# Planning four head-sum steps of block 1 later, one of them past the last LN2 apply of block 0

## The chip, the cores and the metric

The kernel runs on one core of one Trainium2 chip. The metric is device time in microseconds (us) of one execution. TensorE is the matrix engine (PE in the profile, its weight loads PEld), VectorE is DVE, ScalarE is ACT, GpSimd is POOL, and SyncE (SP) issues nearly all DMAs here (517 of 521 by the profile's list). PSUM is the memory that this kernel's matmuls write; the six buffers of its `acc` tiles are called banks here.

## The reference, cut to what matters

```python
x = A_x                                  # 2048 tokens x 1024, bfloat16
x = x + A_ref(layernorm(x), wqkv, wo)    # local dilated attention, 32 heads, 8 keys each
x = x + B_ref(layernorm(x), Wg, Wu, Wd)  # h = relu(gate) * up, 3584 wide, then down
x = x + A_ref(...)                       # both once more, same weights
x = x + B_ref(...)
```

The kernel works on blocks of 512 tokens. Four blocks for the first layer pair and four for the second make eight "blocks" n = 0 to 7. While TensorE runs the gate-up of block n, VectorE computes the attention of block n+1.

## The kernel before

Every piece of work is a closure with a planned time. They are emitted in the order of those times, and most of VectorE's work is chained in that order (`dv` issues each after the last). The planned time is thus only an order: nothing waits for a clock.

The attention scores of one block are a "head sum": products q*k over eight channel groups c, added up, in two halves h. A step is one product and one addition:

```python
def mult(h, c):                # one head-sum step; t has 2 buffers, ac has 1
    def f():
        ...
        dv(nc.vector.tensor_tensor, t[:], i0, i1, op=ALU.mult)   # product
        if c > 1:
            add(h, c - 1)                                        # sum of the step before
        if c == KC - 1:
            add(h, c)
    return f
# steps: [mult(h, c) for h in range(2) for c in range(8)]; so step 6 is h=0, c=6
```

LN2 of block 0 normalizes four tiles; the gate-up of block 0 needs all four, transposed by DMA. Tiles 1 to 3 are done on VectorE: statistics, then `rstd` on GpSimd (a pow), then the apply.

```python
nc.gpsimd.tensor_tensor(rstd[:], vpe[:], neg_half[:, 0:1], op=ALU.pow)   # in the statistics
...
dv(nc.vector.tensor_scalar, xn[:, t, :], x_tile, mv[:, 0:1], rstd[:],    # the apply
   op0=ALU.subtract, op1=ALU.mult)
```

The gate-up allocates its PSUM tiles from six banks; `relu(gate)` has three buffers `r`, and VectorE's multiply `hT` frees both the up bank and an `r`:

```python
for nm in ("g", "u"):
    acc = psum.tile([P, BLK], F32, tag="acc", name=f"acc_{nm}")      # 6 banks
    ... 8 matmuls of 128x128 by 128x512 ...
    if nm == "g":
        rs[j] = pool["hid"].tile([P, BLK], BF16, tag="r", name="r", bufs=3)
        nc.scalar.activation(rs[j][:], acc[:], ACT.Relu)
def gate(j):
    dv(nc.vector.tensor_tensor, hold["hT"][:, j, :], ups.pop(j)[:], rs.pop(j)[:], op=ALU.mult)
```

Weights come in 1 MB slabs through five buffers. The kernel chains what SyncE issues in the order of the plan (`sp_dma`), their loads with nearly all other transfers: `store_s` and `load_s`, which take the head sums through DRAM, stand in this queue too.

Of the kernel before, what the change touches and what calls it, by code (L numbers as in the profile page):

```python
# [36 lines left out]
def kernel(  # L37
# [553 lines left out]
    def prod_sum_steps(n):  # L591
        st = att[n]

        def mult(h, c):
            def f():
                if h == 0 and c == 0:
                    st["s"] = big_tile([P, TPB, W, P], f"s_{n}")
                i0, i1 = qk_bcast(n, c, WH * h, WH)
                if c == 0:
                    t = work.tile([P, WH, BLK], F32, tag="ac", name=f"ac_{n}_{h}", bufs=1)  # L600
                    st["ac"] = t
                else:
                    t = work.tile([P, WH, BLK], F32, tag="t", name=f"t_{n}_{h}_{c}")
                    st[("t", c)] = t
                if n < NB:
                    dv(nc.vector.tensor_tensor, t[:], i0, i1, op=ALU.mult)
                else:
                    nc.vector.tensor_tensor(t[:], i0, i1, op=ALU.mult)  # L608
                if c > 1:
                    add(h, c - 1)  # L610
# [4 lines that stand above are left out]
        def add(h, c):  # L615
            ac, t = st["ac"], st.pop(("t", c))
            o, i0, i1 = ac[:], ac[:], t[:]
            if c == KC - 1:
                o = _ap(st["s"], WH * h * P, [[P, WH], [W * P, TPB], [1, P]])
                i0, i1 = (i[:].rearrange("p w (q t) -> p w q t", t=P) for i in (ac, t))  # L620
            if n < NB:
                dv(nc.vector.tensor_tensor, o, i0, i1, op=ALU.add)
            else:
                nc.vector.tensor_tensor(o, i0, i1, op=ALU.add)  # L624

        return [mult(h, c) for h in range(2) for c in range(KC)]
# [258 lines left out]
    def spread(steps, at, gap):  # L885
        for i, f in enumerate(steps):
            ev.append((at + gap * i, f))
# [37 lines left out]
    t_fill = t_wo0 + GRP * KC  # L925
# [54 lines left out]
    sums1 = prod_sum_steps(1)  # L980
    spread(sums1[:4], t_pv0 + 34.5, 4.5)
    spread(sums1[4:6], t_wo0 + 0.5, 2.5)
    spread(sums1[6:10], t_fill + 1.4, 4.6)
    spread(sums1[10:], t_gu0 + 2.6, 5.4)
    spread(load_v_steps(1), t_wo0 + 4.0, 7.0)
    ev.append((t_gu0 - 0.01, start_hidden))
# [107 lines left out]
```

## Time and profile before

| | before |
|---|---|
| median of three executions | 1617.8 us |
| the profiled execution, a further one, as timed | 1618.55 us |
| its span in the profile | 1616.8 us |
| PE busy | 1610.6 us |
| granted clock | 1.00 |

The profile page of the kernel before, its busy times (engine, us, share of the span, instructions) and the chain of work that ended last:

```profile
PE 1610.6 (100%) x7689; PEld 789.5 (49%) x7689; DVE 1138.9 (70%) x964; ACT 473.4 (29%) x964; POOL 180.5 (11%) x168
...
PE 99%; DMA 1%; DVE 0%; ACT 0%; issue 0%; POOL 0%; DVEq 0%; SPq 0%; ACTq 0%
```

The waits of PE in the kernel before (who waited for whom: total us, times, longest). This is the whole list:

```profile
PE scratch L132 <- DVE ones L309: 1.5, 1, 1.5
PE tp L386 <- DVE xn_first L106: 0.6, 1, 0.6
PE acc_wo L132 <- DMA w_o<-in_A_wo_dram: 0.6, 1, 0.6
```

PE lacked work for 2.7 us, all before 162 us, and the change acts at 180 us. While it works, its groups of eight matmuls start every 1.7263 us, 215.8 ns for each matmul, and of the gate and up groups that the timeline of this trace lists whole, none starts sooner than 1.72 us after the one before it. With no wait left where the change acts, the question is whether it makes a new one; it cannot remove one.

The timeline of VectorE in the kernel before, at the change (start, duration, operation):

```profile
180.24 0.15 DVE L106 TENSOR_SCALAR vpe<-mv 128x1 f32<-128x1 f32 x1
180.32 2.29 DVE L106 TENSOR_TENSOR t<-q,k 128x2048 f32<-128x2048 bf16 x1
182.53 2.28 DVE L106 TENSOR_TENSOR ac<-ac,t 128x2048 f32<-128x2048 f32 x1
184.73 0.54 DVE L106 TENSOR_SCALAR xn_b<-x,mv,rstd 128x1024 bf16<-128x1024 bf16 x1
...
200.85 1.28 DVE L106 TENSOR_TENSOR hT<-acc_u,r 128x512 bf16<-128x512 f32 x2
```

`vpe` is the variance of tile 3, `t` and `ac` the product and sum of step 6, `xn_b` the apply, and the first two `hT` come at 200.85. GpSimd's pow for tile 3, in its timeline:

```profile
180.48 2.54 POOL L300 TENSOR_TENSOR rstd<-vpe,neg_half 128x1 f32<-128x1 f32 x1 [3.49 <-DVE vpe L106]
```

It takes 2.54 us beside the product, against 0.55 us for each of tiles 1 and 2. The timeline of PE, with the first gate and up groups (no idle bracket: no wait):

```profile
190.45 1.89 PE L132 MATMUL acc_g<-xnT_b,w_g 128*128 128x512 bf16 x8
192.17 1.89 PE L132 MATMUL acc_u<-xnT_b,w_u 128*128 128x512 bf16 x8
```

The fifth gate group (starting at 204.26) takes the PSUM bank that the first `hT` frees. And the fifth up slab is issued, and first used, here (SyncE's timeline, then PE's):

```profile
236.78 0.39 SPq L121 DMA_DIRECT2D w_u<-in_B_W_up_dram  x1
...
247.43 1.89 PE L132 MATMUL acc_u<-xnT_b,w_u 128*128 128x512 bf16 x8
```

This load landed 9.2 us after issue by the trace, at 246.0: 1.4 us before its first use.

### The profile page before, as it was taken

To read this page: it belongs to the slowest core of one execution; us is meant where nothing else is said; L and a number is where in the kernel's file an instruction comes from. 1 tells how busy PE (TensorE), PEld (TensorE's weight loads), DVE (VectorE), ACT (ScalarE), POOL (GpSimd) and SP (SyncE) were. 2 spreads that over 40 slices of the span, in tenths; PEclk is the share of its full clock that TensorE was granted. 3 is DMA by queue.
4 is the path that set the end of the run, shared out by engine and by line. 5 is a ranking of instruction groups with operands and counts; after the bars stand their busy time and mean duration, and the time that the engine had idled before them with its cause. 6 is when DMAs were issued, how large, how long until landed. Compare 5 with 4: busy or idle time off the path is not lost.

```text
span 1616.8 us, 19042 instructions
## 1 busy us (share of the span) xinstructions
PE 1610.6 (100%) x7689; PEld 789.5 (49%) x7689; DVE 1138.9 (70%) x964; ACT 473.4 (29%) x964; POOL 180.5 (11%) x168
## 2 busy tenths in 40 slices
PE   9999999999999999999999999999999999999999
PEld 6646544444444445444454444544445444444445
DVE  6999979996989698929389293893939939311211
ACT  4753312132116313603136031361313311131110
POOL 3400100010003002300053000530005100000000
DMA  9767857596659666784747847489574874655452
GB/s 308 180 189 249 213 165 254 183 216 204 208 192 226 192 184 211 192 246 147 227 158 201 241 153 229 154 202 255 161 229 156 206 240 156 210 162 175 156 169 66
DMA packets 359065, 317.94 MB, mean 197 GB/s; under 512 B 105024, under 2 KB 332736, under 8 KB 358464
## 3 DMA queue, kind: packets, MB, share of 16 engines
q1 hardware_dynamic: 358272, 315.87, 67.2%
q8 instruction: 60, 0.98, 0.3%
q10 hardware_dynamic: 704, 0.85, 0.2%
q14 instruction: 29, 0.24, 0.1%
HBM read 266.29 MB, written 34.66 MB: 186 GB/s over the span
## 4 chain that ended last, share of the span: by engine, by line
PE 99%; DMA 1%; DVE 0%; ACT 0%; issue 0%; POOL 0%; DVEq 0%; SPq 0%; ACTq 0%
PE acc_u L132 24%; PE acc_g L132 24%; PE dacc L132 18%; PE acc_v L132 7%; PE acc_q L132 7%; PE acc_wo L132 7%; PE acc_k L132 6%; PE dacc_pair L132 6%; DMA w_o<-in_A_wo_dram 1%; DMA x<-in_A_x_dram 0%; PE tp_pair L386 0%; DVE x L848 0%; DVE bst L103 0%; DVE bst L106 0%; ACT kst L540 0%
## 5 line engine op out<-in xcount | busy, mean ns | idle before, releaser
L132 PE MATMUL acc_u<-xnT_b,w_u 128*128 128x512 bf16 x1792 | 423.3, 379 | 0.0
L132 PE MATMUL acc_g<-xnT_b,w_g 128*128 128x512 bf16 x1792 | 423.3, 379 | 0.0
L793 ACT ACTIVATE r<-acc_g 128x512 bf16<-128x512 f32 x224 | 133.6, 596 | 728.7 <-PE acc_g L132 699.4
L106 DVE TENSOR_TENSOR hT<-acc_u,r 128x512 bf16<-128x512 f32 x224 | 150.9, 686 | 241.7 <-PE acc_u L132 239.1
L132 PE MATMUL dacc<-w_d,hT 128*128 128x512 bf16 (+2 forms) x1428 | 302.0, 371 | 0.0
L132 PEld LDWEIGHTS <-hT 128*128 128x128 bf16 x1876 | 181.3, 98 | 206.0
L132 PEld LDWEIGHTS <-w_u 128*128 128x128 bf16 x1792 | 175.3, 98 | 211.4
L132 PEld LDWEIGHTS <-w_g 128*128 128x128 bf16 x1792 | 175.3, 98 | 211.4
L106 DVE TENSOR_TENSOR pv<-a,vhm 128x4096 bf16<-128x4096 bf16 x64 | 143.5, 2284 | 0.0
L848 DVE TENSOR_TENSOR x<-dacc,x 128x512 bf16<-128x512 f32 (+2 forms) x39 | 24.5, 659 | 154.3 <-PE dacc L132 154.3
L608 DVE TENSOR_TENSOR t<-q,k 128x2048 f32<-128x2048 bf16 x56 | 128.0, 2292 | 6.7 <-ACT k L543 4.6
L106 DVE TENSOR_TENSOR t<-q,k 128x2048 f32<-128x2048 bf16 x56 | 127.5, 2286 | 3.7 <-ACT k L543 2.6
L106 DVE TENSOR_TENSOR pv<-pv 128x1024 bf16<-128x1024 bf16 (+1 forms) x128 | 113.7, 950 | 0.0
L132 PE MATMUL acc_wo<-w_o,oT 128*128 128x512 bf16 x512 | 112.0, 379 | 0.6 <-DMA w_o<-in_A_wo_dram 0.6
L549 POOL COPY kh<-k 128x14 bf16<-128x14 bf16 x40 | 56.0, 1405 | 504.1 <-ACT k L543 504.1
L624 DVE TENSOR_TENSOR ac<-ac,t 128x2048 f32<-128x2048 f32 x48 | 109.7, 2284 | 0.3
L106 DVE TENSOR_TENSOR ac<-ac,t 128x2048 f32<-128x2048 f32 x48 | 109.7, 2284 | 0.0
L263 POOL TENSOR_TENSOR st_b<-st_b,neg_half 128x1 f32<-128x1 f32 x29 | 43.9, 1521 | 526.6 <-ACT st_b L262 526.6
L132 PE MATMUL dacc_pair<-w_d,hT 128*128 128x512 bf16 (+1 forms) x448 | 95.9, 366 | 0.0
L132 PEld LDWEIGHTS <-oT 128*128 128x128 bf16 x512 | 50.0, 98 | 61.2 <-DMA w_o<-in_A_wo_dram 1.1
L258 ACT ACTIVATE xn_b<-x 128x1024 bf16<-128x1024 bf16 x29 | 30.3, 1045 | 127.8 <-DVE x L106 65.7
L446 ACT CAST vT<-acc_v 128x512 bf16<-128x512 f32 x56 | 32.7, 586 | 57.3 <-PE acc_v L132 56.3
(136 smaller groups left out, 1228.0 us busy)
## 6 DMA issues: line engine op xcount, KB each, us to landing
w_g<-in_B_W_gate_dram SPq DMA_DIRECT2D x56, 1024.0 KB, 7.4
w_u<-in_B_W_up_dram SPq DMA_DIRECT2D x56, 1024.0 KB, 5.5
w_d<-in_B_W_down_dram SPq DMA_DIRECT2D x48, 1024.0 KB, 6.2
w_o<-in_A_wo_dram SPq DMA_DIRECT2D x16, 1024.0 KB, 8.1
vhm<-v_d SPq DMA_DIRECT2D x32, 284.0 KB, 6.7
v_d<-vT SPq DMA_DIRECT2D x8, 1024.0 KB, 10.0
oT<-o_d SPq DMA_DIRECT2D x32, 256.0 KB, 3.7
w_d<-in_B_W_down_dram SPq DMA_DIRECT2D x16, 512.0 KB, 3.9
```

What stands on the lines that cost most here:

```text
L106: tail_dve[0] = f(*args, **kwargs).ins
L132: tail_pe[0] = nc.tensor.matmul(*args, **kwargs).ins
L258: nc.scalar.activation(xn, xt[:], ACT.Square, accum_out=sq)
L263: nc.gpsimd.tensor_tensor(rstd, vpe, neg_half[:, 0:1], op=ALU.pow)
L446: tail_act[0] = nc.scalar.copy(st["vT"][:, c, :], acc[:]).ins
L549: nc.gpsimd.tensor_copy(khalo[n][:, c, :], k[:, BLK:BLK + HALO])
L608: nc.vector.tensor_tensor(t[:], i0, i1, op=ALU.mult)
L624: nc.vector.tensor_tensor(o, i0, i1, op=ALU.add)
L793: tail_act[0] = nc.scalar.activation(rs[j][:], acc[:], ACT.Relu).ins
L848: run = dv if n < NB - 2 else (lambda f, *args, **kwargs: f(*args, **kwargs))
```

## The change

The intent: let the last LN2 apply, which gate-up waits for, go ahead of head-sum work that nobody needs soon. The whole diff:

```diff
-    spread(sums1[6:10], t_fill + 1.4, 4.6)
+    spread(sums1[6:10], t_fill + 3.3, 4.0)
```

Tile 3's statistics are planned at `t_fill + 0.1` and its apply at `t_fill + 3.1`. Of the four shifted steps only step 6 crosses another event. Compared in the built programs, PE's order, waits and PSUM banks do not change; on VectorE one apply moves ahead of one product and one sum.

## The prediction

> What bounds the kernel. TensorE is the whole span. The page shows PE busy 1610.6 of 1616.8 us (100%), the chain of waits is 99% PE, and the granted clock is 1.00. Groups of eight 128x512 matmuls start every 1.7263 us in the timeline (215.8 ns each)[...]. The waits of PE list 2.7 us in all: 1.5 (first ones), 0.6 (first transpose), 0.6 (a wo slab, at 161 us). From 165 us to the end the list of PE's waits is empty. Nothing after that point is left for a schedule to win.
>
> What the change does. Compared instruction by instruction, the programs have the same instructions, PSUM banks, TensorE order and TensorE waits. Only one thing moves: on VectorE the LN2 apply of tile 3 (0.54 us) now comes before the product (2.29 us) and sum (2.28 us) of head-sum step 6, instead of after. The other shifted steps keep their places.
>
> Costs, from the timeline at 180 us. Before, the apply's rstd (a POOL pow) is waited for under those two operations: variance at 180.24, product 180.32, sum 182.53, apply 184.73 to 185.27, transpose issued 185.30 and landed 3.2 us later at 188.5. The first gate-up matmul starts at 190.45 without waiting, so the old order had about 1.9 us of slack. After, the apply waits for the pow as tiles 1 and 2 do (0.73 and 0.66 us idle), runs at about 181.1 and ends at about 181.7. Its transpose goes out when the queue gets to it, an estimate of 184 to 185, no later than before: 0.5 to 1.5 us more slack where there was enough. The pow itself, 2.54 us beside the product in the old order and 0.55 us for tiles 1 and 2, should be about 0.55 us again[...].
>
> The price: those 0.7 to 0.8 us of VectorE idle push all later VectorE work back (step 7 from 185.19 to about 186.0, the first gate multiply hT from 200.85 to about 201.6), until VectorE's idle time at 232 to 243 us (2.8 us before each hT) absorbs it. Does PE feel it? By the programs' PSUM banks, the matmul group that starts at 204.26 needs the first hT, which ended at 201.53: 2.7 us of slack, the smallest of this stretch; the others have 2.9 to 6.6 us. The relu that takes the first r buffer again, at 202.73, has 1.2 us. All exceed 0.8. The head-sum halves reach DRAM about 0.8 us later, and the head sum starts at 243.12 behind an hT, with attention's output not needed before 311 us. So on the critical path: 0.0 us.
>
> Prediction: 1617.8 us, unchanged; range 1617.2 to 1618.6 (8 in 10), which is run-to-run scatter (before: 1617.72 to 1617.87) and a small stall unseen. Chances: faster by over 2% 0.00, within 2% 0.99, slower by over 2% 0.01.
>
> What would show it right: PE waits the same 2.7 us, none after 165 us; the gate-up's first matmul still at 190.45; apply 3 at about 181.1 with 0.7 us idle on POOL rstd; that pow near 0.55 us; first hT 0.7 to 0.8 us later; hT back on its old times by 235 us.
>
> What would make it wrong: an earlier transpose that collides with other DMA and lands after 190.4; a slack in PSUM or the r buffers smaller than read; a VectorE delay that lasts past 232 us and reaches block 1's output projection at 311 us; or a chip with another scatter.

The forecast's sum, 0.0 us on the critical path, keeps all its terms: PE's empty list of waits, the 0.7 to 0.8 us of idle, and the slacks of 1.9, 2.7 and 1.2 us. That the pow would take 0.55 us rests on tiles 1 and 2 alone.

## The result, and the profile after

| | before | after |
|---|---|---|
| median (6 executions each) | 1618.03 us | 1618.16 us |
| lowest to highest | 1617.72 to 1618.36 | 1617.87 to 1618.61 |

The ratio is 1.0001 (95% interval 0.9988 to 1.0014): the same. Ratios here are the mean time of one kernel's fast runs over that of the other's in the same rounds, so not quite the ratio of the medians quoted.

All of PE's waits after the change:

```profile
PE scratch L132 <- DVE ones L309: 1.5, 1, 1.5
PE tp L386 <- DVE xn_first L106: 0.2, 1, 0.2
```

Nothing waits after 165 us, as before. The wait of 0.6 us for a `w_o` slab is gone from this trace, but that is not the change's doing: the programs are identical up to there. It makes PE 0.68 us earlier at 190 us than in the trace of the kernel before, and the times of the two profiled executions (1617.87 against 1618.55) differ by just that. The trace of the kernel before is thus of a rather late execution. Compare times of the two traces with that in mind.

VectorE at the change:

```profile
180.35 0.15 DVE L106 TENSOR_SCALAR vpe<-mv 128x1 f32<-128x1 f32 x1
181.16 0.55 DVE L106 TENSOR_SCALAR xn_b<-x,mv,rstd 128x1024 bf16<-128x1024 bf16 x1 [0.66 <-POOL rstd L300]
181.62 2.28 DVE L106 TENSOR_TENSOR t<-q,k 128x2048 f32<-128x2048 bf16 x1
183.83 2.29 DVE L106 TENSOR_TENSOR ac<-ac,t 128x2048 f32<-128x2048 f32 x1
...
201.81 1.28 DVE L106 TENSOR_TENSOR hT<-acc_u,r 128x512 bf16<-128x512 f32 x2
```

The apply runs 3.6 us earlier, and VectorE pays 0.66 us of idle for it, since the pow is no longer hidden. GpSimd's pow and the first gate group on PE:

```profile
180.58 0.55 POOL L300 TENSOR_TENSOR rstd<-vpe,neg_half 128x1 f32<-128x1 f32 x1 [3.49 <-DVE vpe L106]
...
189.77 1.89 PE L132 MATMUL acc_g<-xnT_b,w_g 128*128 128x512 bf16 x8
```

The transpose of tile 3 went out at 183.66 instead of 185.30 us and landed by 187.5 instead of 188.5, in front of a matmul that did not wait in either trace. The first `hT` is 0.96 us later. Two things got closer to a wait. ScalarE's relu waits for an `r` buffer, from the list of all waits of each kernel, before:

```profile
ACT r L793 <- DVE hT L106: 3.3, 1, 3.3
```

and after:

```profile
ACT r L793 <- DVE hT L106: 23.3, 7, 4.9
```

And the fifth up slab after the change, on SyncE and on PE:

```profile
238.45 0.39 SPq L121 DMA_DIRECT2D w_u<-in_B_W_up_dram  x1
...
246.75 1.89 PE L132 MATMUL acc_u<-xnT_b,w_u 128*128 128x512 bf16 x8
```

It landed 7.9 us after issue, at 246.35: 0.4 us of slack where there had been 1.4. Not all of this is the change's: the slab was issued 1.67 us later, PE is 0.68 us earlier in this trace, and a transfer that was 1.3 us faster gave most of it back. With the 9.2 us of the trace before it would have landed 0.9 us after its first use (an estimate from these figures).

One measure leaves out all that differs ahead of the change: the time from PE's first gate-up group to its last group of all. Its last group starts here, before and after:

```profile
1612.54 1.05 PE L132 MATMUL dacc<-w_d,hT 128*128 128x256 bf16 x12
```

```profile
1611.87 1.05 PE L132 MATMUL dacc<-w_d,hT 128*128 128x256 bf16 x12
```

That makes 1422.09 us before (from 190.45) and 1422.10 us after (from 189.77). This measure is called the stretch below. An earlier transpose could win only ahead of it, and there is nothing: from the start of the k groups ahead of the gate-up, at 173.18 and 172.51, to its first group are 17.27 and 17.26 us, ten groups at PE's spacing. It shows in one trace what the scatter of the times hides.

### The profile page after: what moved, and what is told of

It reads as the page before. It is cut to its first block, busy times and chain, and to the rows that moved or that the text cites. A ratio compares the mean times of both kernels' runs of the same rounds, so it can differ in the third digit from the quotient of the medians.

```text
span 1616.2 us, 19042 instructions
## 1 busy us (share of the span) xinstructions
PE 1611.0 (100%) x7689; PEld 789.7 (49%) x7689; DVE 1139.0 (70%) x964; ACT 473.4 (29%) x964; POOL 178.5 (11%) x168
## 4 chain that ended last, share of the span: by engine, by line
PE 99%; DMA 0%; DVE 0%; issue 0%; SPq 0%; ACT 0%; DVEq 0%
PE acc_u L132 24%; PE acc_g L132 24%; PE dacc L132 18%; PE acc_v L132 7%; PE acc_k L132 7%; PE acc_q L132 7%; PE acc_wo L132 7%; PE dacc_pair L132 6%; DMA x<-in_A_x_dram 0%; PE tp_pair L386 0%; DVE x L848 0%; PE L L132 0%; DVE xnT_first L106 0%; PE tp L386 0%; DVE xn_first L106 0%
```

## The experiments

Three theories were put up before the runs. S (slack): the earlier transpose and the later VectorE each stay inside a slack of PE, so neither shows. C (cancel): both show, and they cancel. I (indifferent): VectorE's order never matters here. A fourth, D, came out of the first runs. The four groups of runs (the first four, the next three, the next four, the last) were on different chips, each with its own runs of the kernel before. No kernel here computes anything wrong: the useless VectorE work writes a scratch tile.

### The changed kernel again

No edit.

> The changed kernel once more, with more rounds. Theory S (slack: nothing the change moves is on TensorE's path): ratio to before 1.000, within 0.0003; TensorE's waits empty after 165 us. Theory C (cancel: an earlier transpose wins about 0.8 us and the later VectorE loses about 0.8 us) also says 1.000. Theory I (indifferent: the order on VectorE never matters here) says the same; the next runs tell them apart.

Measured: 1618.77 us median (5 runs, 1617.68 to 1618.99) against 1618.03 for before (9 runs, 1617.62 to 1618.86), ratio 1.0003 (0.999 to 1.0015). PE's waits were again 1.5 and 0.2 us, both early. The means differ by 0.5 us (1618.53 to 1618.07), too little for the interval; a third set is below. The stretch is 1422.09 us (189.57 to 1611.66), as in the kernel before. But the slab was at the edge in this trace: issued at 238.45, it landed at 246.35, 0.2 us before its first matmul at 246.55, and the weight load ahead of that matmul did wait for it, as the timeline of the weight loads (PEld) shows:

```profile
246.38 1.56 PEld L132 LDWEIGHTS <-w_u 128*128 128x128 bf16 x8 [0.17 <-DMA w_u<-in_B_W_up_dram]
```

The matmul itself was not late.

### The delay without the earlier apply

To the kernel before, right after tile 3's apply:

```diff
+    def spend():
+        xt = x_tiles[3]
+        for w in (512, 128):
+            junk = stat_pool.tile([P, 6], F32, tag="junk", name="junk")
+            dv(nc.vector.bn_stats, junk[:], xt[:, 0:w])
+    ev.append((t_fill + 3.2, spend))
```

> The kernel before, with the apply of tile 3 in its old place and about 0.8 us of useless VectorE work (two bn_stats, 512 and 128 wide) right after it: the loss of the change without its earlier transpose. S: 0.0 us (within 0.3), first hT near 201.6 us as in the changed kernel, no TensorE wait after 165 us, more relu waits for hT as in the changed kernel. C: 0.8 us slower than before. I: 0.0.

Measured: 1618.12 us median, ratio 1.0000 (0.9987 to 1.0012). The added work took 0.88 us, and the relu waits for `hT` rose to 17.4 us in 5 waits. The interval alone, about 2 us either way, could not exclude C's 0.8 us. The trace does: PE's list has no wait after the start, and the stretch is 1422.25 us, 0.16 us more than before. One detail pointed ahead: the fifth up slab was issued at 238.4 and landed after 8.8 us, at 247.2, and its first group started at 247.26, 0.14 us later than PE's spacing of 1.73 us would have it. PE's list of waits did not show it; in the list of all waits the weight load waits 0.5 us for the slab.

### The apply between product and sum

```diff
                 dv(nc.vector.tensor_tensor, t[:], i0, i1, op=ALU.mult)
+                if (n, h, c) == (1, 0, 6):
+                    ev3[0]()            # the apply of tile 3, not issued at t_fill + 3.1 any more
                 if c > 1:
                     add(h, c - 1)
```

(The diff is cut to its core and shown at the call.)

> The apply stands between the product and the sum of step 6: earlier than before by one sum, with most of the wait for the pow hidden under the product. The pow should take about 2.5 us again beside the product (as in the kernel before), so the apply waits about 0.3 to 0.5 us and starts near 183.0 us. S: 0.0 us (within 0.3). C: faster than before by 0.3 to 0.8 us. I: 0.0.

Measured: 1617.80 us median, ratio 0.9999 (0.9986 to 1.0012). The timelines of VectorE and GpSimd in this run:

```profile
182.99 0.55 DVE L106 TENSOR_SCALAR xn_b<-x,mv,rstd 128x1024 bf16<-128x1024 bf16 x1 [0.44 <-POOL rstd L300]
...
180.41 2.54 POOL L300 TENSOR_TENSOR rstd<-vpe,neg_half 128x1 f32<-128x1 f32 x1 [3.48 <-DVE vpe L106]
```

The pow took 2.54 us again as soon as a product ran beside it, and the apply waited 0.44 us for it, where it had waited 0.66: the bubble is partly hidden. The times (means 0.16 us below the kernel before, standard error 0.17) can't exclude C's 0.3 us, but the trace does: the k groups ahead of the gate-up take 17.26 us here too, and the stretch is 1422.10 us. Nothing was won, and nothing could be, as PE's first gate-up group did not wait in the kernel before. So C has lost both its halves.

### A fourth relu buffer

```diff
-rs[j] = pool["hid"].tile([P, BLK], BF16, tag="r", name="r", bufs=3)
+rs[j] = pool["hid"].tile([P, BLK], BF16, tag="r", name="r", bufs=4)
```

> The changed kernel with 4 buffers for the relu output r instead of 3. The new waits of ScalarE for hT (23.3 us in 7 waits after the change, 3.3 us in 1 before) should fall to 5 us or less. S: the time stays as it is (within 0.3 us), since PSUM banks hide the late relus. If these waits cost anything, this run is faster than the changed kernel by it. The pool hands out PSUM banks a little differently in this build.

Measured: 1618.16 us median, ratio 1.0000 (0.9986 to 1.0014). The relu waits for `hT` fell from 23.3 us in 7 waits to 2.9 us in 1. Against the changed kernel in the same rounds (1618.77, means 0.45 us apart with a standard error of 0.28) the times leave open whether a few tenths were won; the stretches don't, 1422.10 us here and 1422.09 there. The most visible new wait of the changed kernel cost nothing in these traces.

### Two steps ahead of the apply

To the kernel before:

```diff
-    spread(sums1[6:10], t_fill + 1.4, 4.6)
+    spread(sums1[6:8], t_fill + 1.4, 0.8)
+    spread(sums1[8:10], t_fill + 10.6, 4.6)
```

> The kernel before with steps 6 and 7 of the head sum both ahead of the apply of tile 3: 6.9 us more VectorE work before it, so the apply starts near 191.6 us and its transpose lands near 195. S: TensorE stands at the first gate-up matmul (190.45 us before) for 4.5 to 5.2 us, and the time rises by about that, to 1622.3 to 1623.5 us; the transfers of k queued behind the transpose may add up to 2 us. C: the rise equals the whole delay of the transpose, about 6.9 us. I: no rise.

Measured: 1625.91 us median against 1617.89, ratio 1.0050. I falls: the place of the apply matters as soon as the transpose is late enough. PE's timeline in this run:

```profile
195.43 3.57 PE L132 MATMUL acc_g<-xnT_b,w_g 128*128 128x512 bf16 x8 [5.50 <-issue]
198.79 2.29 PE L132 MATMUL acc_u<-xnT_b,w_u 128*128 128x512 bf16 x8
200.93 1.89 PE L132 MATMUL acc_g<-xnT_b,w_g 128*128 128x512 bf16 x8
```

The transpose was issued at 192.25 and landed 3.1 us later, at 195.35; the profile names no releaser for the wait, but the start follows it by 0.1 us. The rise is 8.0 us, more than S said. Against an unstalled start at 189.77 the first group is 5.7 us late, and then two groups run slow: 3.36 and 2.14 us from start to start instead of 1.73, 2.0 us more. Together that is 7.7 us. The time alone would speak for C, whose 6.9 us is nearer than S's range; but the trace has one stop, of S's kind, and then slow matmuls (631 ns where they take 379), while the granted clock averaged 0.77 from 188 to 203 us, and 1.00 from 203 to 213 us. S had the place right and left the slow matmuls out.

### 3.0 and 6.0 us of useless VectorE work

To the changed kernel, the same `spend` with `(512,) * 5` and `(512,) * 10`. The early apply stays where it is.

> The changed kernel with 3.0 us of useless VectorE work (five bn_stats) after the early apply: VectorE is 3.8 to 4.0 us later than in the kernel before, the transpose is not. S: the slack of 2.7 us (the first hT ends 201.5, the fifth gate group starts 204.3 in its PSUM bank) is passed by 1.1 to 1.9 us; TensorE waits that long once, for hT, at that group, and nowhere else; the time rises by 1.0 to 1.9 us. C: the rise is 3.0 to 3.9 us. I: no rise.

> As the last, with 6.0 us (ten bn_stats), VectorE 6.8 to 7.0 us later than in the kernel before. S: one TensorE wait of 4.1 to 5.0 us at the fifth gate group, time up by about that, 3.0 us more than with 3.0 us of work: past the slack each us of VectorE costs one of the kernel. C: rise of 6 to 7 us. I: no rise.

Measured: 1620.61 us and 1624.55 us against 1617.89: 2.7 and 6.7 us more. PE's waits after the start, with 3.0 us of work:

```profile
PE acc_g L132 <- DVE hT L106: 1.8, 1, 1.8
```

and PE's timeline with 6.0 us:

```profile
208.55 3.19 PE L132 MATMUL acc_g<-xnT_b,w_g 128*128 128x512 bf16 x8 [4.74 <-DVE hT L106]
211.57 1.89 PE L132 MATMUL acc_u<-xnT_b,w_u 128*128 128x512 bf16 x8
```

The wait is the one foretold, for `hT`, at the fifth gate group and of the foretold size. The times are above S's range. With 6.0 us the remainder is the slow group (3.02 us to the next, 1.3 us too long; the granted clock averaged 0.83 from 203 to 213 us). With 3.0 us no group is slow. The trace has a second small loss: the up group expected at 248.87 us started at 249.09, when the fifth up slab landed (issued 241.14, 7.9 us). The two make 2.2 us (1.9 from start to start, and 0.2) in an execution of 1620.24 us, the fastest of the four, 2.35 above the median of before; the stretch grew by 2.17 us, so nothing else was lost. With 6.0 us it grew by 6.21 us, which the wait (4.9 us from start to start) and the slow group make up. This gave theory D: the late head-sum half holds SyncE's queue, and with it the slab behind it. (SyncE waited 13.5 us for `s` in this trace with 3.0 us of work, against 10.8 us in the kernel before, and issued the store at 234.21 instead of 230.09 us.) The rise of 6.7 us also lies in C's range; there the trace decides, not the time.

### Weight slabs ahead of the head-sum loads

To the kernel with 3.0 us of work, and to the changed kernel:

```diff
-            ev.append((at + 40.5, load_s(1)))
+            ev.append((at + 42.0, load_s(1)))
```

> 3.0 us of useless VectorE work as before, which raised the time by 2.6 to 2.7 us where one PSUM wait explains 1.9, with the four loads of the head sum's halves moved in the DMA queue behind the two weight slabs that stood after them. Theory D (a second path: the late head-sum half holds the in-order DMA queue, and the fifth up slab behind it lands too late): rise falls to 1.8 to 2.2 us, TensorE waits once, 1.8 us at the fifth gate group, and the up group at 249 us no longer starts late (0.2 us in the trace before). Theory S alone (PSUM is the only slack): nothing changes, 2.6 us.

> The changed kernel with the same reordering of the DMA queue. D: the fifth up slab, issued at 238.4 us in the changed kernel and landed 0.2 to 0.4 us before its first use, is issued near 231 us and lands over 4 us before it; the time is the same as the kernel before or lower by up to 0.3 us (1617.7 to 1618.0), as the changed kernel may lose 0.1 to 0.4 us in some runs there. S: same time as the changed kernel.

Measured: 1624.22 and 1621.23 us against 1618.26, so 6.0 and 3.0 us slower, not faster. This expectation failed in the time. In the changed kernel with slabs first, the slab did come early (issued 233.30, landed 6.3 us later, against 246.7 needed), but the head-sum loads behind two 1 MB slabs landed late (the median landing of the transfers that write or read the head sum there went from 5.2 to 11.9 us). VectorE's timeline there:

```profile
250.56 2.29 DVE L106 TENSOR_TENSOR u<-s 128x2048 f32<-128x2048 bf16 x1 [8.09 <-DMA s<-s_d]
```

In the changed kernel that sum starts at 243.36. The kernel chains VectorE's work in order, so the `hT` behind it are late too (the next at 254.03 us; in the changed kernel at 246.83), and PE's waits become:

```profile
PE acc_u L132 <- DVE hT L106: 2.3, 2, 1.2
...
PE acc_wo L132 <- DVE x L106: 1.0, 1, 1.0
```

These waits are the loss: listed they are 3.3 us, and the stretch grew by 3.8. The two transfers pull against each other, and the order of the kernel before is the better one. Because the edit opened this other wait, the times of these two runs do not test how much of the 2.7 us was the slab. The trace of the first does, which D had asked for: with 3.0 us of work and the slab early (issued 236.44, landed 6.6 us later), the up group came on PE's spacing, at 248.79 after 247.06, while the wait at the fifth gate group stayed (1.8 us). So the 0.2 us there had been the slab.

### 1.2 and 4.2 us of useless VectorE work

`spend` with `(512,) * 2` and `(512,) * 7`, in the changed kernel.

> The changed kernel with 1.2 us of useless VectorE work (two bn_stats). PSUM alone (S): the first hT comes at most 0.2 us too late for the fifth gate group, rise 0.0 to 0.2 us. D: the fifth up slab lands about 1.2 us later than in the changed kernel, where 0.4 us was left; TensorE waits 0.5 to 0.9 us there; rise 0.5 to 1.2 us. C (no slack): rise 1.2 to 2.1 us.

> The changed kernel with 4.2 us of useless VectorE work (seven bn_stats). With 6.0 us the fifth gate group waited 4.7 us and then ran slow (3.0 us to the next group instead of 1.7)[...]. Here the wait should be 2.9 to 3.1 us: S and D: no slow group, next group 1.73 us later, rise 3.1 (S) or 3.2 to 4.0 us (D, with a late slab); if it runs slow, the slow groups come with any wait of 3 us. C: rise 4.2 to 5.1 us.

Measured with 1.2 us: 1619.70 us median against 1618.26, ratio 1.0007 (0.9995 to 1.002). The five runs fall in two groups, 1618.49 and 1618.60, and 1619.70 to 1619.85. The profile fell in the slower group, and PE's list of waits has the line that D asked for:

```profile
PE acc_u L132 <- DMA w_u<-in_B_W_up_dram: 1.1, 1, 1.1
```

The slab was issued at 239.43 and took 9.1 us. At the fifth gate group PE lost 0.15 us only. The rise, 1.4 us by the medians and 1.1 by the means, is at the upper end of D's range or in C's (1.2 to 2.1), so the time doesn't decide; the trace does. The stretch grew by 1.45 us, of which 1.29 us is the late slab (3.02 us from start to start instead of 1.73) and the rest the gate group. So PSUM alone (S: at most 0.2 us) is not the tightest slack; the slab is. That the two groups come from its landing time is likely, as other traces show 7.9 us, but only one execution of this kernel was traced.

Measured with 4.2 us: 1622.49 us, ratio 1.0028, so 4.2 us more: above the ranges of S and D and at the foot of C's. PE's timeline:

```profile
206.44 2.73 PE L132 MATMUL acc_g<-xnT_b,w_g 128*128 128x512 bf16 x8 [2.93 <-DVE hT L106]
208.97 2.77 PE L132 MATMUL acc_u<-xnT_b,w_u 128*128 128x512 bf16 x8
211.58 1.89 PE L132 MATMUL acc_g<-xnT_b,w_g 128*128 128x512 bf16 x8
```

The wait is as foretold, but the expectation of no slow group failed: two groups lost 1.7 us together. With the 3.1 us by which the gate group was late that is 4.8 us, the whole growth of the stretch, so again the trace speaks for one stop and the slow groups behind it, not for C. The granted clock averages 0.83 from 203 to 213 us in this run too, and 1.00 in the same stretch of the changed kernel with slabs first, where PE did not wait there.

### The changed kernel a third time

No edit.

> The changed kernel a third time, on whatever chip is given, for the few tenths that the first two sets left open (means 0.2 and 0.5 us above the kernel before). D (the fifth up slab has 0.4 us left and its landing time differs by 1.2 us between traces, 7.9 to 9.2): mean 0.2 to 0.5 us above before, and where the traced execution has a landing near 9 us it shows a late up group at 247 us, by up to 0.8 us. S (nothing lost): mean within 0.1 us of before.

Measured: 1618.29 us median (5 runs, mean 1618.32) against 1618.16 (9 runs, mean 1618.19), ratio 1.0001. The means differ by 0.13 us, between what S (at most 0.1) and D (0.2 to 0.5) had said. The traced execution had the slab at 238.80 plus 7.9 us, 0.5 us before its use at 247.20, and no late group. Over the three sets, 16 runs of the changed kernel average 1618.34 us and 24 of the kernel before 1618.11 (standard deviations 0.38 and 0.30): 0.23 us more, with a standard error of 0.11 (0.38/sqrt 16 and 0.30/sqrt 24, added in squares). That would fit a slab that is sometimes late by some tenths, but no trace of the changed kernel shows a late group: the three stretches are 1422.10, 1422.09 and 1422.10 us against 1422.09 before, and the times of these four executions (1617.68 to 1618.55) differ only by when gate-up starts (189.57 to 190.45). For the executions that were not traced it stays open, and it is 0.014%.

## Why the prediction was right

- **"On the critical path: 0.0 us", and 1617.8 us in 1617.2 to 1618.6.** Right: 1618.16. PE had no wait to remove after 165 us and got none.
- **One swap on VectorE and nothing else.** Right, by the built programs.
- **Apply at about 181.1, 0.7 us of idle, pow back to 0.55 us.** Right: 181.16, 0.66 and 0.55. The partly hidden variant made the pow 2.54 us again.
- **The transpose goes out at 184 to 185 us.** At 183.66, a little earlier. Its slack of 1.9 us was real: 6.9 us more work ahead of the apply made PE wait 5.5 us, and two slow groups (2.0 us) did the rest.
- **"The first hT 0.7 to 0.8 us later."** It measured 0.96 us, or 0.85 us after taking off the 0.11 us by which this trace was already later at `vpe`: a little mis-sized.
- **"2.7 us of slack, the smallest of this stretch."** This step failed. For PSUM it holds: the wait at the fifth gate group came where it was computed. But the prediction counted PSUM banks and relu buffers and dismissed the DMA path ("the head-sum halves reach DRAM about 0.8 us later"). Behind that store in the same queue stands the fifth up slab, with 1.4 us of slack before the change and 0.2 to 0.5 in three traces after it. The verdict was right with less room than was claimed, and with some luck: the slab took 7.9 us in all three traces, and with the 9.2 us of the trace before it would have been late in each of them.
- **"The relu ... has 1.2 us. All exceed 0.8."** Failed as well: in the trace PE was 0.68 us earlier and VectorE 0.96 us later, and relu waits for `hT` went from 1 to 7. They cost nothing that a trace shows: the stretch is the same with the fourth buffer.
- **"VectorE's idle time at 232 to 243 us absorbs it."** Mostly: by 238.39 `hT` waits 2.76 us for PE again. The head sum did not start "behind an hT" but waited 0.82 us for its DMA, 0.24 us later than before (243.36 against 243.12).

The cancelling of gain and loss is ruled out by the stretches of the two runs that take the change apart (the delay alone costs 0.16 us of C's 0.8, the earlier apply wins nothing), and indifference by the run with two steps ahead of the apply.

## What to carry to other kernels

When one engine has no waits left, a reordering on another engine can at best change nothing; judge it by the slack that it uses up, and look for slack on every path that the delayed work feeds, in-order DMA queues included. Here a VectorE delay of 1 us was hidden, but it put off the issue of a weight slab by 1.7 us and left 0.2 to 0.5 us of slack, because a store of VectorE's result stood ahead of the slab in one queue (SyncE waited 12.5 us for that result instead of 10.8). The same slab, where it kept its place in the queue, landed 7.6 to 9.2 us after issue, a spread larger than that slack. Past the slack, a long wait of TensorE cost more than its length: after waits of 2.9, 4.7 and 5.5 us the matmuls ran slow for a while, which cost 1.7, 1.3 and 2.0 us more; after one of 1.8 us they did not, and nothing between 1.8 and 2.9 us was tried. An instruction's time here depended on what ran beside it: the pow on 128x1 took 2.54 us beside a 2.29 us product (the kernel before, the delay alone, the split) and 0.55 us while VectorE waited for it (tiles 1 and 2, and tile 3 after the change). Where times scatter by more than the effect, compare traces from the point at which the change acts to the end.
